# Windowed attention with a two-layer MLP: Q and K of two batches turned from 96 partitions, one block of tokens split in two

## The chip, the cores and the metric

The kernel runs on one core of a Trainium2 chip. The metric is the device time of one execution in microseconds (us). The median of several runs is compared with the median of the kernel before.

## What is computed

```python
def _attn_ref(q, k, v):                      # each (8, 8, 576, 64): batch, head, position, width
    scores = q @ k^T / sqrt(64)
    mask = |i - j| <= 32                     # a band of 65 positions
    attn = softmax(where(mask, scores, -1e9))
    return attn @ v

def reference(q, k, v, w_in, w_out, s, b):   # w_in (512, 2048), w_out (2048, 512)
    x = attention, heads side by side        # (4608, 512) tokens by model width
    r = max(x @ w_in, 0)
    return (s * r * r + b) @ w_out           # (4608, 512), float32
```

Inputs and output are float32; the kernel multiplies in bfloat16 and adds up in float32.

## The kernel before

**Order.** The program is a list of tasks, each for one engine, with a planned cost, a key and the tiles that it reads and writes. `_Graph.plan` simulates the engines and the DMA rings with these costs and writes down one fixed order for each engine; `emit` puts the semaphore waits in. Each engine then runs its list strictly in that order, so a task at the head of an engine's list that waits holds up all behind it. Tasks that write the same tile keep the order in which the program adds them.

**The start (batch 0).** SyncE issues eight loads of 288 KB (`load_pair`, line 579): Q and K of a pair of heads, one partition per nine positions of one head (`ROWS = 9`), so 128 partitions of 576 floats. Each load is cast to bfloat16 (`turn_pair`, lines 588 and 589: K on VectorE, Q on ScalarE or GpSimd), turned on TensorE by 18 transposes of 64x64 into a bank of `W` (line 595), and copied into `QT` by ScalarE (line 600) or `KT` by VectorE (line 601). `pair_scores` first writes the band's mask into the score bank with matmuls of an identity with `NEG` (line 817, two of 512 columns; for pair 0 also two in `AVN`, line 822), adds the scores of the pair (line 826, 18 matmuls on a quarter of the array) and lets ScalarE take the exponential (line 848). Before any of this, `WARM = 26` matmuls of 128x128 ones run on TensorE (line 486).

**Units.** Attention goes on in units of 128 rows: `av_part` (line 742, up to 32 matmuls of 64x64), `finish` (reciprocal 764, scaling 766, four transposes 773, copy into `XT` 781). Batch 0 has five units, batch 1 five; `BANK1` names the PSUM tile in which each unit of batch 1 gathers its result. From batch 2 on, Q and K are turned by DMA instead (lines 625 to 650).

**The MLP.** Tokens go in blocks (`sizes`): 96, 128, 128, 160 (the `NE = 4` early ones), then 512 each. For a block `s1` multiplies 128 columns of `w_in` at a time (line 973), ScalarE takes the ReLU (980) and VectorE the square (982). `group(m)` says how many chunks share a bank of `W`: four up to 128 tokens, two up to 256, one above. `s2` is the second layer (line 991; for the early blocks line 1022), 128 tokens at a time. The early blocks' `s1` are taken in the order of `FIRST`, weight group by weight group, as the weights arrive and GpSimd casts them (line 537). `attend(m)` adds attention tasks to the list until 1024 tokens past block `m` are made, so those of all of batch 1, and of batch 2 and part of 3, come into the list ahead of the `s1` of the first block of 512 (tokens 512 to 1023).

Of the kernel before, what the change touches and what calls it, by code (L numbers as in the profile page):

```python
# [11 lines left out]
S = 576  # L12
D = 64
# [19 lines left out]
          ("v", 0), ("v", 1), ("v", 2), ("v", 3), ("v", 4))  # L33
SWITCH = 215.0
XTS = 4000.0
ROWS = 9
XPE = 20
PACE = ((-1, -1, -1),) * 3
CASTS = 40.0
# [2 lines left out]
SLACK = (1000.0, 2000.0, 3000.0, 3000.0)  # L42
PACEV = ((-1,-1,0,0,1),(0,0,1,1,2),(0,0,1,1,2))
EV0 = ("pool", "dve", "pool", "dve", "pool")
BANK1 = ("W", "SC", "W", "SC", "AVN")
EV1 = ("pool", "pool", "pool", "pool", "pool")
EV2 = ("dve",) * 5

ACT_TABLE_SET_ID = 6
FAR = 1e38  # L50
TURN_DVE = ()
WARM = 26
LEAST = 2.0 ** -60
AHEAD = {"pe": 48, "act": 180, "dve": 240, "pool": 240}

# [16 lines left out]
class _Graph:  # L72
# [13 lines left out]
    def add(self, stream, fns, cost, reads=(), writes=(), key=0.0, accum=False, dma=None, waits=(),  # L86
            lat=None, slack=0.0):
        if not isinstance(fns, list):
            fns = [fns]
        after = [self.chain] if key < -100 and self.chain else []  # L90
        t = _Task(len(self.tasks), stream, fns, cost, self.LAT[stream] if lat is None else lat, key,
                  dma, slack, after)
        t.deps.update(waits)
        for a in after:
            assert a.stream == stream
            a.next.append(t)
        for r in reads:
            assert r in self.writer, r
            t.deps.add(self.writer[r])
        for w in writes:  # L100
            if w in self.writer:
                t.deps.add(self.writer[w])
            if not accum:
                t.deps.update(self.readers.get(w, ()))
        t.deps.discard(t)
        for r in reads:
            self.readers.setdefault(r, []).append(t)
        for w in writes:
            self.writer[w] = t
            if not accum:  # L110
                self.readers[w] = []
        self.tasks.append(t)
        if key < -100:
            self.chain = t
        return t
# [201 lines left out]
def bass_sliding_window_symmetric__then__act_starrelu_kernel(  # L317
# [10 lines left out]
    B = q.shape[0]  # L328
    T = B * S

    sizes = [96, 128, 128, 160]
    NE = len(sizes)
    while sum(sizes) < T:
        sizes.append(min(512, T - sum(sizes)))
    TBLK, t0 = [], 0
# [5 lines left out]
    with ExitStack() as es:  # L341
# [24 lines left out]
        STG = [STGS[:, i, :] for i in range(NSTG)]  # L366
        NATS = sb((128, NNAT, 2 * DM), BF16, "nat")
        NAT = [NATS[:, i, :] for i in range(NNAT)]
# [112 lines left out]
        for p0 in (0, 64):  # L481
# [1 line left out]

        add("pool", lambda e: e.tensor_scalar(NEG[:, :], MASK[:, :], 1.0, FAR, ALU.subtract, ALU.mult), 250,
            reads=[("MASK", 0, 0), ("MASK", 0, 64)], writes=["NEG"], key=-95.5)
        add("pe", [lambda e: e.matmul(W[:, 1, 0:128], lhsT=ONESW[:, :], rhs=ONESW[:, :], start=True, stop=True)] * WARM,
            110.0 * WARM, reads=["ONESW"], writes=[("W", 1)], key=-99)

        def mask_of(c, u):

# [84 lines left out]
        def load_pair(b, name, pr, load_key):  # L575

            si = take("stg", NSTG)
            land["pair", b, name, pr] = si
            add("sp", lambda e: e.dma_start(  # L579
                STG[si][:, 0:576],  # L580
                src_of[name][b, 2 * pr:2 * pr + 2, :, :].rearrange("h (p i) d -> (h p) (i d)", i=ROWS)),
                600.0, writes=[("STG", si)], key=load_key, dma=("l", 8, 113.0 if b == 0 else 93.0))

        def turn_pair(b, name, pr, key, banks, eng, slack):

            slot, si, ni = b % 2, land["pair", b, name, pr], take("nat", NNAT)
            nat = NAT[ni][:, 0:576]
            add(eng, (lambda e: e.copy(nat, STG[si][:, 0:576])) if eng == "act" else
                (lambda e: e.tensor_copy(nat, STG[si][:, 0:576])),
                {"act": 670.0, "dve": 420.0, "pool": 700.0}[eng], reads=[("STG", si)], writes=[("NAT", ni)],  # L590
                key=key, slack=slack)
            res, tile = banks[take("bank", len(banks))]
            view = tile.bitcast(BF16)[:, 0:S].rearrange("p (i s) -> p i s", i=ROWS)
            order = view.rearrange("p i s -> p s i")
            add("pe", [lambda e, i=i, p0=p0: e.transpose(  # L595
                view[p0:p0 + 64, i, :], nat[p0:p0 + 64, i * 64:i * 64 + 64], IDENT[p0:p0 + 64, p0:p0 + 64])
                for i in range(ROWS) for p0 in (0, 64)], 500.0, reads=[("NAT", ni), "IDENT"], writes=[res], key=key)
            flat = QT[slot][:, pr, WIN:WIN + S] if name == "q" else KT[slot][:, pr, :]
            dst = flat.rearrange("p (s i) -> p s i", i=ROWS)
            add(*(("act", lambda e: e.copy(dst, order), 190 + 0.833 * S) if name == "q" and (b, pr) not in TURN_DVE else  # L600
                  ("dve", lambda e: e.tensor_copy(dst, order), 60 + 1.04 * S)), reads=[res],
                writes=[({"q": "QT", "k": "KT"}[name], slot, x, pr) for x in range(NTILE)], key=key)
# [205 lines left out]
        def pair_scores(b, pr):  # L808


            name, bank = (("SC", SC), ("O", O))[pr % 2 if b == 0 else 0]
            whole = range(NTILE - NTILE % 2)
            tail = [NTILE - 1] if b == 0 and NTILE % 2 else []
            if b == 0:
                wide = NEG.rearrange("p (one c) -> p one c", one=1)
                four = wide.to_broadcast((128, 4, 128))
                add("pe", [lambda e, hp=hp: e.matmul(bank[:, hp, :].rearrange("p (a c) -> p a c", a=4), lhsT=IDENT[:, :],
                                                     rhs=four, start=True, stop=True, skip_group_check=True)
                           for hp in (0, 1)], 440, reads=["NEG", "IDENT"], writes=[(name, 0), (name, 1)], key=-80.0 + pr)
                if pr == 0:  # L820
                    half = wide[0:64].to_broadcast((64, 4, 128))
                    add("pe", [lambda e, hp=hp: e.matmul(
                        AVN[0:64, hp, :].rearrange("p (a c) -> p a c", a=4), lhsT=IDENT[0:64, 0:64],
                        rhs=half, start=True, stop=True, skip_group_check=True) for hp in (0, 1)],
                        440, reads=["NEG", "IDENT"], writes=[("AVN", 0), ("AVN", 1)], key=-79.5)
            fns = [lambda e, j=j, hp=hp: e.matmul(  # L826
                bank[64 * (j % 2):64 * (j % 2) + 64, hp, 64 * (j - j % 2):64 * (j - j % 2) + 128] if j in whole else
                AVN[0:64, hp, pr * 128:pr * 128 + 128],
                lhsT=KT[b][64 * hp:64 * hp + 64, pr, 64 * j:64 * j + 64],
                rhs=QT[b][64 * hp:64 * hp + 64, pr, 64 * j:64 * j + 128], start=b > 0, stop=True,  # L830
                skip_group_check=True)
                for j in list(whole) + tail for hp in (0, 1)]
# [52 lines left out]
        def attention():  # L885
# [41 lines left out]
            for u in range(NUNIT):  # L927
# [2 lines left out]
                    exp_mask(1, u, due(1, u) - 3.0)  # L930
                last.append((1, u))
                close()
            yield 2 * S
            for b in range(PAIRS, B):
                c = seq_of(b)
                later(b, due(c, group_of(b)[0]) - 24.0)
# [22 lines left out]
        def group(m):  # L959
            return 4 if TBLK[m][1] <= 128 else 2 if TBLK[m][1] <= 256 else 1  # L960
# [84 lines left out]

        def attend(m):
            nonlocal made
            while made < min(T, TBLK[m][0] + TBLK[m][1] + 1024):
                made = next(units)

        made = next(units)
# [2 lines left out]
                s1(m, ft)  # L1054
        early()
        attend(NE)
        for ft in range(16):
            s1(NE, ft)

        def second(m):  # L1060
# [3 lines left out]

        for m in range(NE + 1, NM):
            attend(m)
            for ft in range(16):
                s1(m, ft)
            second(m - 1)
        *rest, final = subs(NM - 1)  # L1070
# [249 lines left out]
```

## Time and profile before

| what | value |
|---|---|
| runs of the kernel | 318.11, 318.45, 319.67 us (median 318.45) |
| the profiled execution, its own time | 316.62 us |
| its span in the profile | 314.9 us |
| TensorE busy | 303.8 us (96%), 3559 matmuls and as many weight loads |
| VectorE, ScalarE, GpSimd busy | 189.6, 140.6, 90.5 us |
| DMA moved | 56.13 MB |

The span is what the profiler's records cover; the execution's own time has 1.7 us around it. "PE" is TensorE's matmuls, "PEld" its weight loads, "DVE" VectorE, "ACT" ScalarE, "POOL" GpSimd and "SP" SyncE. PEclk is the share of the clock that TensorE was granted.

### The profile page before, as it was taken

How to read it: one execution, taken by the hardware profiler on the slowest of the kernel's cores; microseconds unless marked ns; L12 is line 12 of the kernel's file. 1: busy time of each engine (PE TensorE's matmuls, PEld its weight loads, DVE VectorE, ACT ScalarE, POOL GpSimd, SP SyncE). 2: the span in 40 equal slices, each digit the busy share in tenths (PEclk: the TensorE clock that was granted, in tenths of full speed). 3: DMA queues.
4: the chain of work that ended last, by engine and by line, in shares of the span. 5: the costliest groups of instructions: out<-in, count | busy, mean ns of one | idle time of the engine just before them, and what ended most of it. 6: DMA issues, size and time to landing. Idle time of an engine off the chain costs nothing.

```text
span 314.9 us, 8371 instructions
## 1 busy us (share of the span) xinstructions
PE 303.8 (96%) x3559; PEld 158.6 (50%) x3559; DVE 189.6 (60%) x376; ACT 140.6 (45%) x219; POOL 90.5 (29%) x106
## 2 busy tenths in 40 slices
PE   7689999999999999999999999999999999999996
PEld 5478864544554544544444444444444444444444
DVE  2457686598886796686588666856455543333312
ACT  3636536257635765644354445444444333333300
POOL 7366853743334217142321601333000000000000
PEclk9959999999999999999999999999999999999999
DMA  7999999979998998999999799996211110010022
GB/s 252 296 278 392 386 311 301 187 151 312 233 152 242 242 165 199 287 162 139 269 225 186 180 220 291 143 181 129 72 54 52 52 46 34 33 37 33 34 88 83
DMA packets 98985, 56.13 MB, mean 178 GB/s; under 512 B 74048, under 2 KB 88128, under 8 KB 98944
## 3 DMA queue, kind: packets, MB, share of 16 engines
q1 hardware_dynamic: 98944, 55.56, 75.4%
q8 instruction: 29, 0.48, 0.7%
q14 instruction: 12, 0.10, 0.1%
HBM read 36.70 MB, written 9.44 MB: 147 GB/s over the span
## 4 chain that ended last, share of the span: by engine, by line
PE 86%; DMA 6%; DVE 3%; SPq 2%; issue 1%; ACT 1%
PE w L973 38%; PE o L991 33%; DMA stg<-in_k_dram 5%; PE avn L742 4%; PE o L1022 2%; PE avn L1022 2%; PE sc L684 2%; DMA vst<-in_v_dram 1%; SPq L625 1%; PE sc L742 1%; PE w L595 1%; PE avn L773 1%; SPq L579 1%; DVE xn L766 1%; PE sc L826 1%
## 5 line engine op out<-in xcount | busy, mean ns | idle before, releaser
L973 PE MATMUL w<-xt,win 128*128 128x512 bf16 (+3 forms) x768 | 145.5, 330 | 0.1
L980 ACT ACTIVATE r<-w 128x512 bf16<-128x512 f32 (+2 forms) x148 | 86.6, 586 | 104.9 <-PE w L973 90.9
L991 PE MATMUL o<-wout,gt 128*128 128x512 bf16 (+1 forms) x528 | 126.7, 373 | 0.0
L982 DVE TENSOR_TENSOR gt<-r 128x512 bf16<-128x512 bf16 (+2 forms) x148 | 77.4, 529 | 80.4 <-ACT r L980 79.7
L973 PEld LDWEIGHTS w<-xt,win 128*128 128x128 bf16 x768 | 63.5, 100 | 55.8 <-ACT r L980 0.8
L991 PEld LDWEIGHTS o<-wout,gt 128*128 128x128 bf16 x528 | 51.1, 98 | 57.3 <-DVE gt L982 0.2
L633 POOL CAST nat<-stg 128x1024 bf16<-128x1024 f32 (+1 forms) x21 | 25.3, 1204 | 64.6 <-DMA stg<-in_q_dram 47.8
L650 POOL COPY kt<-ktr 128x512 bf16<-128x512 bf16 (+1 forms) x30 | 31.8, 1060 | 38.2 <-DMA ktr<-nat 36.7
L712 ACT ACTIVATE ex<-sc 128x1024 bf16<-128x1024 f32 (+1 forms) x29 | 29.6, 1022 | 22.7 <-PE avn L742 21.6
L1007 DVE SCALAR_TENSOR_TENSOR outs<-o,sb,cvec 128x512 f32<-128x512 f32 (+1 forms) x35 | 25.4, 728 | 11.7 <-PE o L991 11.7
L716 DVE TENSOR_TENSOR ex<-ex,mask 128x1024 bf16<-128x1024 bf16 (+1 forms) x29 | 21.8, 752 | 1.1
L766 DVE TENSOR_TENSOR xn<-avn,rec 128x512 bf16<-128x512 f32 (+1 forms) x30 | 20.6, 688 | 0.9
L742 PE MATMUL avn<-vb,ex 64*64 64x65 bf16 x920 | 19.5, 199 | 0.7 <-DVE ex L716 0.5
L742 PEld LDWEIGHTS avn<-vb,ex 64*64 64x64 bf16 x920 | 12.7, 108 | 13.9 <-issue 6.1
L571 DVE CAST vb<-vst 128x512 bf16<-128x512 f32 (+1 forms) x30 | 12.9, 435 | 1.7 <-DMA vst<-in_v_dram 1.7
L633 DVE CAST nat<-stg 128x1024 bf16<-128x1024 f32 (+1 forms) x15 | 11.7, 786 | 1.2 <-DMA stg<-in_k_dram 1.2
L684 PE MATMUL sc<-qt,kt 64*64 64x128 bf16 x440 | 11.7, 216 | 0.7 <-ACT xt L781 0.7
L764 DVE RECIPROCAL rec<-avn 128x8 f32<-128x8 f32 (+1 forms) x30 | 6.0, 201 | 7.6 <-PE avn L742 7.3
L537 POOL CAST win<-stg 128x1024 bf16<-128x1024 f32 x8 | 8.4, 1049 | 6.4 <-DMA stg<-in_moe_w_in_dram 6.4
L537 POOL CAST wout<-stg 128x1024 bf16<-128x1024 f32 x8 | 8.8, 1100 | 2.0 <-DMA stg<-in_moe_w_out_dram 1.7
L781 ACT COPY xt<-avn 128x512 bf16<-128x512 bf16 (+2 forms) x13 | 6.6, 519 | 5.9 <-PE avn L773 5.9
L1022 PE MATMUL o<-wout,gt 128*128 128x512 bf16 x32 | 9.3, 381 | 0.0
(88 smaller groups left out, 143.0 us busy)
## 6 DMA issues: line engine op xcount, KB each, us to landing
out_dram<-outs SPq DMA_DIRECT2D x35, 256.0 KB, 2.9
vst<-in_v_dram SPq DMA_DIRECT2D x32, 256.0 KB, 6.6
stg<-in_q_dram SPq DMA_DIRECT2D x6, 1024.0 KB, 6.5
stg<-in_k_dram SPq DMA_DIRECT2D x6, 1024.0 KB, 10.8
stg<-in_moe_w_in_dram SPq DMA_DIRECT2D x8, 512.0 KB, 7.0
stg<-in_moe_w_out_dram SPq DMA_DIRECT2D x8, 512.0 KB, 9.7
stg<-in_q_dram SPq DMA_DIRECT2D x8, 288.0 KB, 5.5
stg<-in_k_dram SPq DMA_DIRECT2D x8, 288.0 KB, 5.4
```

Of the source, the lines that this page charges most:

```text
L633: add(eng, lambda e, x=x: e.tensor_copy(nat[0:top, 1024 * x:1024 * x + 1024].rearrange("p (i h d) -> p h i d", h=H, i=2), stg[0:top, :].re ...
L650: add("pool", lambda e, c=c, w=w: e.tensor_copy(KT[slot][:, :, c:c + w].rearrange("p a (s i) -> p a s i", i=4), KTR[slot][:, :, :, c // 4: ...
L712: add("act", lambda e, dst=flat_dst, src=flat_src: e.activation(dst, src, AF.Exp, bias=0.0, scale=0.125), 190 + 0.833 * 512 * len(hs), rea ...
L716: add("dve", lambda e, flat=flat, mask=mask: e.tensor_tensor(flat, flat, mask, ALU.mult), 130 + 0.53 * 512 * len(hs), reads=[("E", ei, hp, ...
L742: return [lambda e: e.matmul(av[64 * x:64 * x + 64, h, 0:D + 1], lhsT=buf[64 * g:64 * g + 64, h % 2, h // 2, c:c + 64], rhs=VB[64 * g:64 * ...
L766: add("dve", lambda e: e.tensor_tensor(XN[xi][0:p1, :].rearrange("p (a c) -> p a c", a=H), av[0:p1, :, 0:D], REC[ri][0:p1, :].rearrange("p ...
L973: add("pe", [lambda e, g=g, kc=kc: e.matmul(wt[:, g, :], lhsT=WIN_BF[:, kc, (f0 + g) * 128:(f0 + g + 1) * 128], rhs=XT[:, kc, t0 % XR:t0 % ...
L980: add("act", lambda e: e.activation(rt, wt, AF.Relu, bias=0.0, scale=1.0), 190 + 0.833 * ng * nt, reads=[("W", wb)], writes=[("R1", rb)], ...
L982: add("dve", lambda e: e.tensor_tensor(GT[gs][:, f0:f0 + ng, g0:g0 + nt], rt, rt, ALU.mult), 130 + 0.53 * ng * nt, reads=[("R1", rb)], wri ...
L991: add("pe", [lambda e, fc=fc: e.matmul(O[:, ob, 0:cn], lhsT=GT[gs][:, fc, g0:g0 + 128], rhs=WOUT_BF[:, fc, c0:c0 + cn], start=(fc == 0), s ...
L1007: add("dve", lambda e: e.scalar_tensor_tensor(OUTS[us][:, 0:cn], bank, SB128[:, 0:1], CVEC[:, c0:c0 + cn], ALU.mult, ALU.add), 200 + 1.07 ...
L1022: add("pe", [lambda e, fc=fc, bank=bank, gs=gs, g0=g0: e.matmul(bank, lhsT=GT[gs][:, fc, g0:g0 + 128], rhs=WOUT_BF[:, fc, :], start=(fc == ...
```

## The change

Four things are changed together.

1. `ROWS` is 6: Q and K of batches 0 and 1 lie in 96 partitions with both heads of the pair side by side, so a load has 192 pieces of 1536 bytes instead of 128 of 2304, a cast handles 96 x 768 elements instead of 128 x 576 and swaps two dimensions, and a turn is six transposes of 96 x 128 instead of 18 of 64 x 64.
2. The ones-matmuls at the start are five of 512 columns instead of 26 of 128.
3. The mask of pair `pr` (line 817) is kept behind the turn of K of pair `pr - 1`.
4. Tokens 512 to 1023 are two blocks of 256 (`NE` stays 4). The generator gives control back after each unit of batch 1, and the first block of 256 asks for no tokens past itself; units 2 and 3 of batch 1 gather in `SC` and `AVN` instead of `W` and `SC`.

```diff
-ROWS = 9
+ROWS = 6
-BANK1 = ("W", "SC", "W", "SC", "AVN")
+BANK1 = ("W", "SC", "SC", "AVN", "AVN")
-WARM = 26
+WARM = 5
...
-    sizes = [96, 128, 128, 160]
-    NE = len(sizes)
+    sizes = [96, 128, 128, 160, 256, 256]
+    NE = 4
...
-        add("pe", [lambda e: e.matmul(W[:, 1, 0:128], lhsT=ONESW[:, :], rhs=ONESW[:, :], start=True, stop=True)] * WARM,
-            110.0 * WARM, reads=["ONESW"], writes=[("W", 1)], key=-99)
+        ones = ONESW.rearrange("p (one c) -> p one c", one=1).to_broadcast((128, 4, 128))
+        add("pe", [lambda e: e.matmul(W[:, 1, :].rearrange("p (a c) -> p a c", a=4), lhsT=ONESW[:, :], rhs=ones,
+                                      start=True, stop=True)] * WARM,
+            430.0 * WARM, reads=["ONESW"], writes=[("W", 1)], key=-99)
...
-                STG[si][:, 0:576],
-                src_of[name][b, 2 * pr:2 * pr + 2, :, :].rearrange("h (p i) d -> (h p) (i d)", i=ROWS)),
-                600.0, writes=[("STG", si)], key=load_key, dma=("l", 8, 113.0 if b == 0 else 93.0))
+                STG[si][0:S // ROWS, 0:2 * ROWS * D].rearrange("p (h c) -> p h c", h=2),
+                src_of[name][b, 2 * pr:2 * pr + 2, :, :].rearrange("h (p i) d -> p h (i d)", i=ROWS)),
+                600.0, writes=[("STG", si)], key=load_key, dma=("l", 12, 75.0 if b == 0 else 62.0))
...
-            add("pe", [lambda e, i=i, p0=p0: e.transpose(
-                view[p0:p0 + 64, i, :], nat[p0:p0 + 64, i * 64:i * 64 + 64], IDENT[p0:p0 + 64, p0:p0 + 64])
-                for i in range(ROWS) for p0 in (0, 64)], 500.0, reads=[("NAT", ni), "IDENT"], writes=[res], key=key)
+            add("pe", [lambda e, i=i: e.transpose(view[:, i, :], nat[:, i, :], IDENT[0:np_, 0:np_])
+                       for i in range(ROWS)], 300.0 if b else 400.0, reads=[("NAT", ni), "IDENT"], writes=[res], key=key)
+            land["turn", b, name, pr] = g.tasks[-1]
...
                            for hp in (0, 1)], 440, reads=["NEG", "IDENT"], writes=[(name, 0), (name, 1)], key=-80.0 + pr,
+                    waits=[land["turn", 0, "k", pr - 1]] if pr else [])
...
-            yield 2 * S
+                yield closed[0]
...
-            while made < min(T, TBLK[m][0] + TBLK[m][1] + 1024):
+            while made < min(T, TBLK[m][0] + TBLK[m][1] + (1024 if m > NE else 0)):
                 made = next(units)
...
-        for ft in range(16):
+        for ft in range(0, 16, group(NE)):
             s1(NE, ft)
...
-            for ft in range(16):
+            for ft in range(0, 16, group(m)):
                 s1(m, ft)
```

The casts' planned costs are adapted as well (830, 560 and 930 ns for ScalarE, VectorE and GpSimd).

More of the change, by code (lines that the diff above doesn't have):

```diff
@@ L579, in load_pair @@
             add("sp", lambda e: e.dma_start(
-                STG[si][:, 0:576],
-                src_of[name][b, 2 * pr:2 * pr + 2, :, :].rearrange("h (p i) d -> (h p) (i d)", i=ROWS)),
-                600.0, writes=[("STG", si)], key=load_key, dma=("l", 8, 113.0 if b == 0 else 93.0))
+                STG[si][0:S // ROWS, 0:2 * ROWS * D].rearrange("p (h c) -> p h c", h=2),
+                src_of[name][b, 2 * pr:2 * pr + 2, :, :].rearrange("h (p i) d -> p h (i d)", i=ROWS)),
+                600.0, writes=[("STG", si)], key=load_key, dma=("l", 12, 75.0 if b == 0 else 62.0))
         def turn_pair(b, name, pr, key, banks, eng, slack):
             slot, si, ni = b % 2, land["pair", b, name, pr], take("nat", NNAT)
[L587 to L590, printed above, removed]
+            np_, n = S // ROWS, 2 * ROWS * D
+            nat = NAT[ni][0:np_, 0:n].rearrange("p (i c) -> p i c", i=ROWS)
+            dst = NAT[ni][0:np_, 0:n].rearrange("p (i h d) -> p h i d", i=ROWS, h=2)
+            src = STG[si][0:np_, 0:n].rearrange("p (h i d) -> p h i d", i=ROWS, h=2)
+            add(eng, (lambda e, dst=dst, src=src: e.copy(dst, src)) if eng == "act" else
+                (lambda e, dst=dst, src=src: e.tensor_copy(dst, src)),
+                {"act": 830.0, "dve": 560.0, "pool": 930.0}[eng], reads=[("STG", si)], writes=[("NAT", ni)],
                 key=key, slack=slack)
@@ L818, in pair_scores @@
                                                      rhs=four, start=True, stop=True, skip_group_check=True)
-                           for hp in (0, 1)], 440, reads=["NEG", "IDENT"], writes=[(name, 0), (name, 1)], key=-80.0 + pr)
+                           for hp in (0, 1)], 440, reads=["NEG", "IDENT"], writes=[(name, 0), (name, 1)], key=-80.0 + pr,
+                    waits=[land["turn", 0, "k", pr - 1]] if pr else [])
                 if pr == 0:
```

## The prediction

> **What bounds the kernel now.** I read the page first, then the chain of waits, then the windows view of the start, and the timeline where the chain has holes.
>
> From the page:
>
> ```profile
> PE 303.8 (96%) x3559; PEld 158.6 (50%) x3559; DVE 189.6 (60%) x376; ACT 140.6 (45%) x219; POOL 90.5 (29%) x106
> ...
> PEclk9959999999999999999999999999999999999999
> ...
> q8 instruction: 29, 0.48, 0.7%
> ```
>
> TensorE is the bound. It is without work for only 314.9 - 303.8 = 11.1 us, and one slice, the third (15.7 to 23.6 us), ran at half clock. What can be won lies there. The chain of waits, beginning and end of the start:
>
> ```profile
> 3.14 5.41 DMA stg<-in_k_dram
> ...
> 11.93 1.65 issue
> 13.59 0.31 PE sc L826 x8
> ...
> 19.65 1.39 PE w L973 x16
> ...
> 64.90 0.41 PE sc L684 x8
> ```
>
> The loads of Q and K set the pace up to 8.6 us; then there are 1.65 us of "issue", in which TensorE waits for nothing that the profile shows; from 18 us on the chain is nearly all TensorE. The windows view, cut where the clock changes and into thirds of the 10.24 us between two changes:
>
> ```profile
> core 0: us, PE busy (x) PEld busy (x) DVE busy (x) ACT busy (x) POOL busy (x), PEclk, DMA share, GB/s
> 0.00:11.93 11.93, 9.00 (x222) 6.49 (x222) 4.89 (x17) 5.99 (x8) 7.46 (x24) 1.00 0.87 264
> 1.22:4.64 3.42, 2.89 (x27) 2.62 (x28) 0.74 (x7) 1.54 (x2) 2.85 (x9) 1.00 0.78 254
> 4.64:8.05 3.41, 2.81 (x60) 1.36 (x60) 1.25 (x3) 0.69 (x2) 2.35 (x9) 1.00 0.98 347
> 8.05:11.46 3.41, 2.73 (x116) 2.09 (x118) 2.52 (x5) 2.87 (x4) 1.30 (x3) 1.00 1.15 280
> 11.46:14.88 3.42, 1.76 (x56) 0.92 (x54) 1.09 (x2) 1.62 (x3) 0.88 (x2) 1.00 1.04 313
> 14.88:25.12 10.24, 8.87 (x190) 7.05 (x191) 5.25 (x11) 4.65 (x9) 6.67 (x9) 0.50 1.03 293
> 25.12:35.36 10.24, 10.11 (x164) 9.21 (x163) 7.40 (x16) 6.54 (x13) 7.46 (x7) 1.00 1.05 390
> ```
>
> The clock falls to 0.50 at 14.88 us and comes back at 25.12. The first window's 1.00 is not to be believed: the timeline has 26 ones-matmuls of 128 columns in 2.96 us, 110 ns each, where 128 columns later take 56 (below). So TensorE began at half clock, and the ones raised it near 4.64 us. The DMA share near 1 says that the loads are at their limit until 64 us.
>
> ```profile
> 1.12 2.96 PE L486 MATMUL w<-onesw 128*128 128x128 bf16 x26 [1.12 <-DVE onesw L463]
> ...
> 13.59 0.31 PE L826 MATMUL sc<-qt,kt 64*64 64x128 bf16 x8 [1.65 <-issue]
> ...
> 42.75 0.76 PE L595 MATMUL w<-ident,nat 64*64 64x64 bf16 x36
> 43.44 0.60 PE L1022 MATMUL avn<-wout,gt 128*128 128x512 bf16 x2
> ...
> 64.90 0.41 PE L684 MATMUL sc<-qt,kt 64*64 64x128 bf16 x8 [0.68 <-ACT xt L781]
> 65.25 2.76 PE L973 MATMUL w<-xt,win 128*128 128x512 bf16 x12
> ```
>
> **The change part by part.** All sums are against the profiled execution, 316.62 us with a span of 314.9.
>
> *The turns themselves: nothing.* At full clock 36 transposes of 64x64 start within 43.44 - 42.75 = 0.69 us, 19 ns each because two run side by side, 0.345 us a turn. Six whole-array ones go at the rate of line 773, four between 59.45 and 59.68 in the chain, 55 to 58 ns: 0.34 us. The count falls (16 turns x 12 = 192 fewer matmuls, as many weight loads), the time does not. The copies out of `W` keep their size (0.64 and 0.75 us).
>
> *Fewer instructions before the gap: -1.65 us.* The gap comes after 222 matmuls and 222 weight loads, in the middle of one task. The page has 29 instruction packets for 7118 TensorE rows, about 245 a packet, so I read it as the wait for a packet of code, asked for while the loads fill the DMA engines. The change takes 21 ones and, in the eight turns, 96 matmuls away before this point, 234 rows with their loads. The 444th row then lies in the third unit's matmuls (line 742, 18.70 us now), some 7 us later, while the packet starts at most a few us later. Bounds: 0 (the gap reappears there) to -1.65; I take -1.65.
>
> *The cold stretch.* I read the rows so that the clock goes by how much of the array works. I weigh each matmul's columns by its share of the 128x128 array. 11.46 to 14.88 holds 36 score matmuls (a quarter of 128 columns: 1152), two mask matmuls (1024) and 18 transposes (a quarter of 64: 288), 2464 of some 8190 that fit into 3.41 us (512 in 216 ns is about 2400 a us), 0.30; after it the clock fell. The same count gives 0.32 and 0.42 for the two windows before, and there it stayed. At half clock (4096 columns) 18.29 to 21.70 has 0.69 and did not raise it, 21.70 to 25.12 has 0.78 and did, and 25 ones (3200) gave 0.78. After the change the stretch of the fall holds the same scores and mask, a turn of 12 x 96 columns x 0.75 = 864 and, the gap being gone, the first unit's 24 matmuls (390): 3430, 0.42, where it stayed. At full clock the work of 14.88 to 25.12 shrinks: 32 matmuls of line 742 from 0.95 to 0.70 (x4.5: 1.1), four transposes of line 773 from 0.61 to 0.39 (x3.5: 0.8), the two groups of line 973 from 1.46 and 1.89 to about 1.0 each (1.4): 3.3 us.
>
> [...]
>
> *The cap.* Gap and clock together are 4.95 us, but the weights come no sooner. Casts of `w_in` (GpSimd, line 537, idle before each for the DMA) end at 17.4, 23.3, 27.4 and 30.1 us for the four groups; their first uses are at 19.6, 26.3, about 31 and 36.8. The second group allows 3.0 us. So -3.0.
>
> *Loads and casts of 96 partitions.* The eight loads are 2.36 MB, 6.2 us at the 380 GB/s of 6 to 8 us; the 2 KB pieces of the weights ran at 390 (25.12 to 35.36). Pieces of 1.5 KB I bound from 0 to 10% worse, 0 to +0.6 us for all that follows; I take +0.3. K's last cast grows from 0.46 to 0.61 (768 to 576 elements), +0.15, on the path to the last scores. Q's on GpSimd grow by 0.2 beside it.
>
> *The moved masks: 0.* Line 817 of pair 1 (0.53 us) leaves the place ahead of the first turns; the third K load, landing at 8.55, ends last there. Behind its wait stand only scores that need the same turn. Without this cover it would cost 0.53.
>
> *Two blocks of 256.* 64 matmuls of 512 columns become 128 of 256. The chain has eight of 160 columns in 0.55 us (69 ns each) and four of 512 in 0.86 (216 ns), so a fixed part of some 2 ns lies in each, 64 times 2 ns or 0.15 us. Banks still hold 512 columns, so ScalarE's 597 ns and VectorE's 516 come as often. `s1` of the first half needs two units of batch 1, not four: the 0.68 us before 64.90 and 0.32 near 46.5 can be filled. -0.3 to -1.0; I take -0.8. From 66 us on the same work runs on a busy TensorE.
>
> *Given back.* At 41 to 47 us casts of batch 1's Q and K wait for DMA (0.4 to 0.8 us each). TensorE, earlier by up to 3.0, can meet them in its fixed order, with line 1022 as cover. 0 to +3.0; I take +0.5, because line 1022's 64 matmuls (13.8 us) are mostly still to do then.
>
> Sum: -3.0 + 0.3 + 0.15 + 0.15 - 0.8 + 0.5 = -2.7 us, 313.9 on the profiled execution. That one lies 1.8 under the median 318.45 of the runs, and the place of the clock's windows, which differs from run to run, may be why. I put the sum on the median: 315.7, 312.6 to 316.9 with the bounds (low: -4.0 on 316.62).
>
> **The rivals.** *The clock rises late (slower).* Five ones are 2560 columns, 0.62 of 4096: less than the 0.69 that did not raise it. The masks and whole-array turns from 4.6 us on may do it (at half clock 1024 + 256 + 864 + some 600 by 8.05: 0.67) or miss again. It decides if the clock is still at half at about 11.5 us, since then TensorE, not the loads, is behind: five pairs of masks at 0.85, 48 transposes at 110 ns, four times 18 score matmuls at 0.9: 4.3 + 5.3 + 3.7 = 13.2 us from 4.6, 17.8 against the end of the scores at 14.8 now, +3.0. With the other terms 318.45 + 3.0 + 0.6 - 0.8 = 321.2, or 319.4 on the profiled execution. For it: the 0.62. Against it: denser turns, and late rises in the runs of before too.
>
> [...]
>
> *The gap goes, the clock falls as now.* -1.65 + 0.6 - 0.8 + 0.5 = -1.35: 317.1.
>
> *The loads hide it all.* If pieces of 1.5 KB cost the whole 0.6 us and batch 1's loads take the rest back, only the filled holes stay, -0.8 + 0.6: 318.3. This is also the case in which the new turns change nothing.
>
> **How the numbers follow.** Forecast 0.48, gap only 0.22, late clock 0.16, loads 0.14. A difference under 0.5% (1.6 us) cannot be told from none here. Faster (under 316.9): 0.46 of the forecast's and half of the second rival, whose bounds lie on both sides, 0.57. Same: the other half, the loads and a little of the late clock, 0.28. Slower (over 320.0): 0.15. The range 312.8 to 319.8 leaves out the worst of the late clock and the forecast's edge.
>
> **What would show it.** Right: no "issue" of over 1 us before 15 us; PEclk without the 5 in the third slice; the first line 973 group at about 17.5 us and the second weight group's at 23.5; the first 256-wide line 973 rows near 57 us; no new wait of TensorE after 66. Wrong: line 595 matmuls 110 ns apart up to 12 us, scores of pair 3 ending after 15 us, a gap inside line 742 near 18, or TensorE idle for DMA between 40 and 48 us.

## The result and the profile after

| kernel | median of the runs (us) | range | profiled execution, its span |
|---|---|---|---|
| before | 318.54 (4 runs) | 318.11 to 319.67 | 316.62, 314.9 |
| after | 323.61 (4 runs) | 322.12 to 324.12 | 322.12, 320.3 |

The ratio is 1.0146, with an interval of 1.0101 to 1.019: slower by 1.5%, where 315.7 was forecast, and outside the range of 312.8 to 319.8. Ratios here compare runs timed beside each other, without the few that lie over 1.5% above the fastest of their kernel, so they differ a little from the quotient of the medians.

The page of the kernel after: busy time, clock, instruction packets, the chain by engine, and the issues of Q and K of batches 0 and 1 (count, KB each, median us from issue to landing).

```profile
PE 300.6 (94%) x3365; PEld 163.8 (51%) x3410; DVE 192.3 (60%) x376; ACT 140.9 (44%) x219; POOL 94.6 (30%) x106
...
PEclk9857999999999999999999999999999999999999
...
q8 instruction: 28, 0.46, 0.6%
...
PE 74%; DMA 17%; DVE 3%; issue 2%; SPq 1%; POOL 1%; ACT 1%; DVEq 0%
...
stg<-in_q_dram SPq DMA_DIRECT2D x8, 288.0 KB, 8.1
stg<-in_k_dram SPq DMA_DIRECT2D x8, 288.0 KB, 7.6
```

The same rows of before, for loads of the same 288 KB:

```profile
stg<-in_q_dram SPq DMA_DIRECT2D x8, 288.0 KB, 5.5
stg<-in_k_dram SPq DMA_DIRECT2D x8, 288.0 KB, 5.4
```

So a load takes 2.2 to 2.6 us longer from issue to landing, and the share of DMA on the chain has nearly tripled (before has 86% PE and 6% DMA there). (That share alone proves little: the kernel with wide loads below has 13% and about the time of before.) (45 matmul records are missing here, 3365 against 3410 weight loads; the idle pieces of 0.16 us beside groups of seven matmuls come from that, and some of the lower PE share with them.)

The chain of the waits of after, from the stretches 0 to 30 us and 40 to 110 us (start, duration, what):

```profile
4.21 8.92 DMA stg<-in_k_dram
...
13.15 0.56 DVE nat L594
13.71 0.68 DVE kt L606
...
14.43 0.66 PE w L600 x6
...
41.06 9.21 DMA stg<-in_k_dram
...
50.30 0.56 DVE nat L594
50.85 0.67 DVE cvec L1045
...
51.57 0.42 PE sc L832 x16
```

In before, the chain left the DMA at 8.55 us. Here it stays on a load of K until 13.1, and goes back to one from 41 to 50 us. The windows view of 2 to 12 us shows what those loads got; its last two columns are the DMA share and the GB/s. First before, then after:

```profile
2.00:12.00 10.00, 8.13 (x216) 5.60 (x213) 4.06 (x9) 4.86 (x8) 6.30 (x18) 1.00 1.03 314
```

```profile
2.00:12.00 10.00, 8.23 (x62) 3.65 (x61) 3.04 (x6) 3.86 (x6) 5.57 (x17) 1.00 1.05 251
```

The DMA engines are as busy (1.03 and 1.05) and move a fifth less. How the delay goes on is seen from VectorE's casts of K, TensorE's first matmuls of a kind, and the first load of batch 2:

| event | before (us) | after (us) | later by |
|---|---|---|---|
| last cast of K, batch 0 | 10.17 | 13.15 | 3.0 |
| first `s1` matmuls (line 973 before, 979 after) | 19.58 | 22.10 | 2.5 |
| first scores of batch 1 | 46.78 | 51.57 | 4.8 |
| last cast of K, batch 1 | 46.65 | 52.54 | 5.9 |
| first load of batch 2 issued | 47.84 | 54.29 | 6.5 |
| end | 314.9 | 320.3 | 5.4 |

The timeline of TensorE after (start, duration, operation, count, idle time before it):

```profile
1.12 2.32 PE L487 MATMUL w<-onesw 128*128 128x512 bf16 x5 [1.12 <-DVE onesw L463]
...
14.43 0.66 PE L600 MATMUL w<-ident,nat 96*128 96x96 bf16 x6 [1.23 <-DVE kt L606]
...
51.57 0.42 PE L832 MATMUL sc<-qt,kt 64*64 64x128 bf16 x16 [1.09 <-DVE cvec L1045]
...
97.71 0.40 PE L778 MATMUL avn<-ident,xn 128*128 128x128 bf16 x4 [1.02 <-DVE xn L771]
...
103.22 1.90 PE L979 MATMUL w<-xt,win 128*128 128x512 bf16 x8 [0.68 <-ACT xt L786]
...
105.88 0.25 PE L747 MATMUL avn<-vb,ex 64*64 64x65 bf16 x6 [0.76 <-POOL kt L655]
```

Three waits stand near 100 us (1.02, 0.68 and 0.76 us). From 66 to 110 us TensorE was busy for 43.89 of 44 us before and for 40.37 after:

```profile
66.00:110.00 44.00, 43.89 (x540) 21.49 (x539) 34.80 (x63) 27.16 (x43) 16.07 (x16) 1.00 1.00 224
```

```profile
66.00:110.00 44.00, 40.37 (x568) 26.44 (x564) 33.99 (x60) 22.99 (x36) 20.27 (x19) 1.00 0.97 209
```

Of the 3.5 us between the two, the three waits are 2.5; most of the rest is the idle pieces of eight matmuls that are missing from the records in this stretch. So some of the loss shows far behind the place where the change was made. What causes these waits is not shown: batch 2's loads were issued 6.5 us late, but two of the three waits stand also in the kernel with wide loads below, whose batch 2 was issued in time.

How the loads of batch 2 come late is seen from SyncE's queue after:

```profile
34.27 0.33 SPq L581 DMA_DIRECT2D stg<-in_q_dram  x1
...
45.23 8.97 SPq L564 DMA_DIRECT2D vst<-in_v_dram  x5
54.29 0.56 SPq L630 DMA_DIRECT2D stg<-in_q_dram  x1
```

The first load of batch 1 goes out at 34.27 us (31.41 in before), behind the weights. The last load of batch 1 goes out at 44.87 us (40.91 in before). Behind all eight stand five loads of V, which take 8.97 us on the queue, until 54.2 us (6.46 us in before, until 47.7); the longest of the five takes 4.97 us (47.11 to 52.08), and the profile names nothing that released it. Only then comes batch 2.

### The profile page after: what moved, and what is told of

It is laid out like the page before. It is cut to its first block, busy times and chain, and to the rows that moved or that the text cites. A ratio compares the mean times of both kernels' runs of the same rounds, so it can differ in the third digit from the quotient of the medians.

```text
span 320.3 us, 8026 instructions
## 1 busy us (share of the span) xinstructions
PE 300.6 (94%) x3365; PEld 163.8 (51%) x3410; DVE 192.3 (60%) x376; ACT 140.9 (44%) x219; POOL 94.6 (30%) x106
## 4 chain that ended last, share of the span: by engine, by line
PE 74%; DMA 17%; DVE 3%; issue 2%; SPq 1%; POOL 1%; ACT 1%; DVEq 0%
PE w L979 32%; PE o L997 31%; DMA stg<-in_k_dram 9%; PE avn L747 3%; DMA stg<-in_moe_w_out_dram 3%; DMA stg<-in_moe_w_in_dram 3%; DMA ktr<-nat 2%; PE sc L689 2%; PE avn L1028 1%; PE o L1028 1%; SPq L581 1%; PE sc L747 1%; PE sc L832 1%; PE w L600 1%; DVE outs L1013 1%
## 5 line engine op out<-in xcount | busy, mean ns | idle before, releaser
L979 PE MATMUL w<-xt,win 128*128 128x512 bf16 (+4 forms) x813 | 141.1, 315 | 3.7 <-issue 1.4
L997 PE MATMUL o<-wout,gt 128*128 128x512 bf16 (+1 forms) x510 | 122.8, 372 | 2.1 <-issue 1.6
L979 PEld LDWEIGHTS w<-xt,win 128*128 128x128 bf16 x832 | 70.3, 99 | 54.0 <-ACT xt L786 0.8
L997 PEld LDWEIGHTS o<-wout,gt 128*128 128x128 bf16 x528 | 50.4, 98 | 54.8
L655 POOL COPY kt<-ktr 128x512 bf16<-128x512 bf16 (+1 forms) x30 | 32.9, 1097 | 44.4 <-DMA ktr<-nat 42.9
L717 ACT ACTIVATE ex<-sc 128x1024 bf16<-128x1024 f32 (+1 forms) x29 | 29.7, 1023 | 22.7 <-PE avn L747 21.8
L1013 DVE SCALAR_TENSOR_TENSOR outs<-o,sb,cvec 128x512 f32<-128x512 f32 (+1 forms) x35 | 25.4, 729 | 13.2 <-PE o L997 12.9
L771 DVE TENSOR_TENSOR xn<-avn,rec 128x512 bf16<-128x512 f32 (+1 forms) x31 | 21.4, 689 | 0.9
L747 PEld LDWEIGHTS avn<-vb,ex 64*64 64x64 bf16 x952 | 13.1, 108 | 14.1 <-issue 7.0
L573 DVE CAST vb<-vst 128x512 bf16<-128x512 f32 (+1 forms) x30 | 15.2, 505 | 2.4 <-DMA vst<-in_v_dram 2.2
L594 DVE CAST nat<-stg 96x768 bf16<-96x768 f32 x8 | 4.4, 554 | 9.7 <-DMA stg<-in_k_dram 9.7
## 6 DMA issues: line engine op xcount, KB each, us to landing
stg<-in_moe_w_out_dram SPq DMA_DIRECT2D x8, 512.0 KB, 10.2
```

The costliest lines, as they stand in the source:

```text
L655: add("pool", lambda e, c=c, w=w: e.tensor_copy(KT[slot][:, :, c:c + w].rearrange("p a (s i) -> p a s i", i=4), KTR[slot][:, :, :, c // 4: ...
L717: add("act", lambda e, dst=flat_dst, src=flat_src: e.activation(dst, src, AF.Exp, bias=0.0, scale=0.125), 190 + 0.833 * 512 * len(hs), rea ...
L747: return [lambda e: e.matmul(av[64 * x:64 * x + 64, h, 0:D + 1], lhsT=buf[64 * g:64 * g + 64, h % 2, h // 2, c:c + 64], rhs=VB[64 * g:64 * ...
L771: add("dve", lambda e: e.tensor_tensor(XN[xi][0:p1, :].rearrange("p (a c) -> p a c", a=H), av[0:p1, :, 0:D], REC[ri][0:p1, :].rearrange("p ...
L979: add("pe", [lambda e, g=g, kc=kc: e.matmul(wt[:, g, :], lhsT=WIN_BF[:, kc, (f0 + g) * 128:(f0 + g + 1) * 128], rhs=XT[:, kc, t0 % XR:t0 % ...
L997: add("pe", [lambda e, fc=fc: e.matmul(O[:, ob, 0:cn], lhsT=GT[gs][:, fc, g0:g0 + 128], rhs=WOUT_BF[:, fc, c0:c0 + cn], start=(fc == 0), s ...
```

## The experiments

**Theory:** a load into 96 partitions moves fewer bytes a second than one into 128, whatever the size of its pieces, and it sets the pace at both batches. **Rivals:** the pieces of 1536 bytes are to blame; the casts and turns in the new layout; the clock, which rose late (in after only at 10.25 us, and it was back at half from 13.67 to 27.32, 13.65 us against 10.24 in before); the split with its other banks. All ratios are to the kernel before, timed on the same chip beside each. Differences of medians between two changed kernels cross chips; where they matter the difference of the ratios stands beside them.

The long stretch of half clock does not explain the loss. The mean granted clock of the four runs of after is 0.979 in the profiled one (322.12 us) and 0.989 in the other three, the same as in the profiled run of the nine-row kernel below; these three took 323.18 to 324.12 us, longer than the profiled one.

### The loads by themselves

A kernel that does nothing but load Q's and K's first batches, 16 loads of 288 KB in each of eight phases, with a wait between the phases.

```diff
+ phase 1, 8: 128 partitions, one piece of 2304 B        STG[:, 0:576]
+ phase 2:    96 partitions, two pieces of 1536 B        STG[0:96, 0:768], "h (p i) d -> p h (i d)"
+ phase 3:    96 partitions, one piece of 3072 B         STG[0:96, 0:768]
+ phase 4:    128 partitions, two pieces of 1152 B, 128 B apart
+ phase 5:    as phase 2, in partitions 32 to 127
+ phase 6:    two DMAs of 32 partitions (0-31, 32-63), 4608 B each
+ phase 7:    two DMAs of 32 partitions (0-31, 64-95), 4608 B each
```

> This kernel only loads; attention and the MLP are left out. Eight phases, each the 16 loads of 288 KB of Q and K of batches 0 and 1, each phase waiting for the one before: (1) 128 partitions, pieces of 2304 bytes; (2) partitions 0 to 95, two pieces of 1536; (3) partitions 0 to 95, one piece of 3072; (4) 128 partitions, two pieces of 1152; (5) partitions 32 to 127, two of 1536; (6) partitions 0 to 31 and 32 to 63, pieces of 4608; (7) partitions 0 to 31 and 64 to 95, pieces of 4608; (8) as (1). Theory, the number and place of the partitions set the rate: phases 1, 4 and 8 some 380 GB/s (12.4 us for 4.72 MB), phases 2, 3 and 5 all near 270 (17.5 us), phase 6 about half of phase 1, phase 7 near phase 1. Rival, the size of the pieces sets it: phase 2 and 5 near 270, phase 3 near 400, phase 4 the slowest of the first five (about 220), phases 6 and 7 both near 400.

The windows of that kernel, one in the middle of each phase (the last two columns are DMA share and GB/s):

```profile
core 0: us, POOL busy (x), PEclk, DMA share, GB/s
4.00:12.00 8.00, 0.00 (x0) 1.00 1.00 364
20.00:32.00 12.00, 0.00 (x0) 1.00 1.09 244
41.00:53.00 12.00, 0.00 (x0) 1.00 1.02 270
61.00:67.00 6.00, 0.00 (x0) 1.00 1.03 331
77.00:91.00 14.00, 0.00 (x0) 1.00 1.07 249
97.00:115.00 18.00, 0.00 (x0) 1.00 1.03 214
119.00:135.00 16.00, 0.00 (x0) 1.00 0.93 240
143.00:151.00 8.00, 0.00 (x0) 1.00 0.99 367
```

Over whole phases (4.72 MB by the time from the phase's first packet to the end of its last) the eight ran at 333, 238, 261, 324, 236, 211, 250 and 334 GB/s. The second phase is the load of the change, the first that of before: 238 against 333, or 1.40 times as long. Pieces of 1152 bytes in 128 partitions hardly lose (324), one piece of 3072 in 96 partitions does (261): the number of partitions decides, and two pieces in place of one cost about a tenth more within 96. The seventh phase missed its expectation: two DMAs of 32 partitions in different halves got 250, not the rate of 128; the same two in one half (the sixth phase) got 211.

### The loads, by halves of the partitions

The same with other places, to see why 96 is slow.

```diff
+ phase 1: 128 partitions, one DMA
+ phase 2: 64 partitions (0-63), one DMA      phase 3: 64 partitions (64-127), one DMA
+ phase 4: four DMAs of 16 partitions at 0, 64, 16, 80
+ phase 5: four DMAs of 16 partitions at 0, 32, 16, 48
+ phase 6: two DMAs of 64 partitions (0-63, 64-127)
```

> Loads only again (attention and the MLP are left out), 16 of 288 KB a phase: (1) 128 partitions, one DMA a load; (2) partitions 0 to 63; (3) 64 to 127; (4) partitions 0-15, 64-79, 16-31, 80-95 as four DMAs of 16; (5) partitions 0-15, 32-47, 16-31, 48-63 as four DMAs of 16; (6) 0 to 63 and 64 to 127 as two DMAs. [...] Rival, the rate goes with the number of partitions alone: (2) to (5) all between 211 and 250, (6) as (1).

Over whole phases: 348, 205, 206, 155, 126 and 225 GB/s. The windows of phases 1, 2, 3:

```profile
4.00:12.00 8.00, 0.00 (x0) 1.00 1.00 370
20.00:34.00 14.00, 0.00 (x0) 1.00 1.02 209
44.00:58.00 14.00, 0.00 (x0) 1.00 1.03 212
```

Either half of the partitions alone gets 0.59 of the rate of all (205 and 206 of 348). Two DMAs, one to each half, do not add up (225): of these six, only the one DMA across all partitions gets 348. The fourth and fifth phases missed the author's estimates (155 and 126, where 300 or more and 211 were estimated): DMAs of 16 partitions were slow in both places. That the place counts, and not the number of partitions alone, is seen from pairs with equal DMAs in both halves and in one: 155 / 126 = 1.23 here, 250 / 211 = 1.18 in the run before.

At the 205 GB/s of one half, the two thirds of a load into 96 partitions that lie in one half would let the whole run at 205 / (2/3) = 307 GB/s, if the last third cost no time beside them: an estimate from the 205 alone. Measured are 238 and 261, so by this estimate the rate of one half does not explain all of it. What the rest is, no run here shows.

### The changed kernel with the old rows

```diff
 (after)
-ROWS = 6
+ROWS = 9
+load_pair and turn_pair as before: 128 partitions of 576, 18 transposes of 64x64
```

> The changed kernel with its loads, casts and turns of Q and K put back to nine rows in 128 partitions; ones, moved masks and two blocks of 256 stay. Theory, the slower loads of 96 partitions cost the time (k of pair 3 landed 3 us later, and the same again for batch 1): back by 4 to 6 us to 317.5 to 319.5, last K cast of batch 0 at 10.2 us. Rival, the clock's late rise after the shorter ones: the start stays late, first group of the first layer after 21 us, 321.5 to 323.5. Rival, the split of the block makes the waits of TensorE seen between 95 and 106 us: these stay, 320.5 to 322.

Measured: 316.95 us (316.34 to 317.91, 10 runs), ratio 0.9954 (0.992 to 0.9989). Its windows row of 2 to 12 us, the issues of its page, and the wait for K of batch 1 in its timeline:

```profile
2.00:12.00 10.00, 8.65 (x148) 4.52 (x148) 3.28 (x7) 3.53 (x6) 6.19 (x18) 1.00 1.01 302
```

```profile
stg<-in_q_dram SPq DMA_DIRECT2D x8, 288.0 KB, 5.7
stg<-in_k_dram SPq DMA_DIRECT2D x8, 288.0 KB, 5.9
```

```profile
47.40 0.42 PE L830 MATMUL sc<-qt,kt 64*64 64x128 bf16 x16 [0.35 <-DVE cvec L1043]
```

The rows take the whole loss with them and more: 323.61 - 316.95 = 6.7 us, or 6.1 by the ratios; that is better than the theory's range. The last cast of K starts at 10.91 us, against 13.15 in after (10.2 was expected). The three waits near 100 us are gone too, and TensorE is busy for 43.93 of the 44 us from 66 to 110. Its clock rose at 11.24 us only, fell at 18.07 and came back at 24.90, and it is still quicker than before: the late rise is not what cost the time.

### The kernel before with the new rows alone

```diff
 (before)
-ROWS = 9
+ROWS = 6
+load_pair and turn_pair of the change; 26 ones, masks, blocks and banks as before
```

> The kernel before with loads, casts and turns of Q and K from 96 partitions, nothing else changed. Theory of the loads: 322.5 to 324.5, last K cast of batch 0 near 13 us. Rival of the clock: 318 to 319.5 (26 ones are still there). Rival of the split: 318 to 319.5.

Measured: 326.68 us (323.33 to 327.8, 4 runs), ratio 1.0247 (1.0151 to 1.0344). The last cast of K starts at 12.78 us, the first scores of batch 1 wait 1.23 us (1.09 in after):

```profile
12.78 0.56 DVE L592 CAST nat<-stg 96x768 bf16<-96x768 f32 x1 [0.62 <-DMA stg<-in_k_dram]
```

```profile
51.29 0.42 PE L829 MATMUL sc<-qt,kt 64*64 64x128 bf16 x16 [1.23 <-DVE cvec L1042]
```

The rows alone cost 8.1 us on the kernel before, more than the 5.1 of the whole change and more than the theory's range (322.5 to 324.5). The 26 ones that were kept do not prevent it. In the profiled execution the clock fell a second time, from 68.04 to 74.86 us, after waits of TensorE of 0.79, 0.44 and 0.68 us. That fall does not explain the surplus: the mean granted clock is 0.979 in three of the four runs, but the fourth, with 0.989, took 327.80 us, the longest. Why the rows cost more here than in the changed kernel is not shown.

### The changed kernel with wide loads only

The casts and turns stay those of the change (96 x 768, six transposes); only the DMA writes 128 partitions of 576, which puts the values of Q and K into other places.

```diff
 (after)
-STG[si][0:96, 0:768] <- "h (p i) d -> p h (i d)", i=6
+STG[si][:, 0:576]    <- "h (p i) d -> (h p) (i d)", i=9
+memset of STG columns 576:768, once, at the start
```

> The changed kernel, but its loads of Q and K fill 128 partitions with pieces of 2304 bytes as before; casts and turns still work on 96 partitions of 768 elements, so the values of Q and K stand in the wrong places and the rest of each row is zero or old data; the eight small memsets for the zeros lie on an idle VectorE. Theory, the landing of the loads alone costs the time: 316.5 to 318.5, last K cast of batch 0 near 10.3 us. Rival, the longer casts (0.56 and 0.82 us) and the turns carry part of it: 319.5 to 322 with a last K cast near 10.3 us all the same.

Measured: 317.7 us (316.55 to 319.43, 10 runs), ratio 0.998 (0.9951 to 1.0009). From its windows, issues and VectorE's timeline:

```profile
2.00:12.00 10.00, 8.78 (x65) 4.27 (x64) 5.45 (x17) 3.85 (x6) 6.68 (x18) 1.00 1.02 302
```

```profile
stg<-in_q_dram SPq DMA_DIRECT2D x8, 288.0 KB, 5.7
stg<-in_k_dram SPq DMA_DIRECT2D x8, 288.0 KB, 5.7
```

```profile
11.02 0.55 DVE L596 CAST nat<-stg 96x768 bf16<-96x768 f32 x1
```

The landing alone is worth 323.61 - 317.7 = 5.9 of the 6.7 us (5.3 of 6.1 by the ratios). For the new casts and turns (and the memsets that this kernel adds) 0.8 us are left, and the intervals of the two runs overlap. The profiled execution is the slowest of the ten, 319.43 us. In it batch 2's first load goes out at 47.56 us, as early as in before (47.84), and two of the three waits near 100 us are there all the same:

```profile
98.72 1.90 PE L981 MATMUL w<-xt,win 128*128 128x512 bf16 x8 [0.68 <-ACT xt L788]
101.40 0.25 PE L749 MATMUL avn<-vb,ex 64*64 64x65 bf16 x6 [0.78 <-POOL kt L657]
```

One thing was not tried. The plan of after prices a load of batch 0 at 12 x 75 = 900 ns, where before has 8 x 113 = 904, so the engines' fixed orders were made for loads as quick as before. How much of the 5.9 us an order made for the slower loads would save is open.

### Old rows for batch 0 only

```diff
 (after)
+if b == 0: load and turn as in the kernel before (nine rows); else: six rows
```

> The changed kernel with nine rows in 128 partitions for batch 0 alone; batch 1 still loads into 96 partitions. Theory, both batches' loads delay TensorE, each by some 3 us: 319 to 321. Rival, only the start counts since batch 1's loads are hidden behind the early blocks: 316.5 to 318. Rival, the start is made up for later and only batch 1 counts: 322 to 324.

Measured: 320.32 us (318.38 to 324.01, 10 runs), ratio 1.0052 (1.0016 to 1.0088): 3.3 us under after, 3.4 over nine rows in both batches (3.0 and 3.1 by the ratios). The last cast of K of batch 0 is back at 10.36 us, but TensorE still waits for batch 1:

```profile
49.37 0.42 PE L868 MATMUL sc<-qt,kt 64*64 64x128 bf16 x16 [1.56 <-DVE cvec L1081]
```

So each batch pays about half.

### The split alone

```diff
 (before)
-BANK1 = ("W", "SC", "W", "SC", "AVN")
+BANK1 = ("W", "SC", "SC", "AVN", "AVN")
-sizes = [96, 128, 128, 160]
+sizes = [96, 128, 128, 160, 256, 256]     # NE = 4, and part 4 of the change
```

> The kernel before with tokens 512 to 1023 as two blocks of 256, control given back after each unit of batch 1, and the new banks; loads, ones and masks as before. Theory of the loads: 317.5 to 318.8, since the split alone only fills holes near 64 us (at most 1 us). Rival of the split: 320.5 to 322 with waits of TensorE of 0.5 us and more between 90 and 110 us. Rival of the clock: 318 to 319.

Measured: 318.93 us (316.41 to 320.18, 10 runs), ratio 1.0031 (0.9998 to 1.0065). The 0.8 us expected of it do not show, and neither does the rival's loss of 2 us and more. The gap stands at its old place, after 222 matmuls, but is short, since TensorE came to it 1.3 us later (clock up at 10.56 us only, although it had 26 ones); a second one of 0.59 us follows at 19.90, after 348:

```profile
13.48 0.31 PE L826 MATMUL sc<-qt,kt 64*64 64x128 bf16 x8 [0.21 <-issue]
```

### The start: masks, ones, and both

Three kernels from before, one with the moved masks, one with five long ones, one with both; a fourth from the nine-row kernel with eight ones.

```diff
 (before_masks)          +waits=[land["turn", 0, "k", pr - 1]] on line 817
 (before_five_ones)      -WARM = 26 (128 columns)   +WARM = 5 (512 columns)
 (before_ones_and_masks) both
 (nine_rows_eight_ones)  in after with nine rows:  -WARM = 5   +WARM = 8
```

> The kernel before with the masks kept behind the turns of K, nothing else. Theory, TensorE's 0.53 us move off the place ahead of the first turn but the loads end last there: 317.5 to 318.6, no difference that can be told. Rival, the moved masks are what made the nine-row version faster: 316.5 to 317.3.

> The kernel before with the five long ones-matmuls alone. Theory of the loads: 317.5 to 318.8, no difference that can be told, as the clock rose late with 26 ones too (10.6 and 16.8 us in two runs). Rival of the clock: 319.5 to 321.

> The kernel before with the five long ones-matmuls and the masks kept behind the turns of K; no split, nine rows. Theory of the loads: these two parts are worth 0 to 2 us, 316.5 to 318.5, since everything but the loads gained 1.6 us. Rival of the clock: too few ones, 319.5 to 321.

> The changed kernel with nine rows in 128 partitions and eight long ones-matmuls instead of five (3.4 us at half clock, ending just before the first masks). If an early rise of the clock is worth something it rises near 4.6 us in more runs: 315 to 316.5. If the rise is only shifted with the fall that follows 7 to 10 us later: as with five, 316.5 to 317.5.

The first rise of the clock is read from the spacing of equal matmuls, the rest from the granted clock of the windows.

| kernel | median (us), runs | ratio | clock up, down, up (us) | gap |
|---|---|---|---|---|
| masks | 319.5, 12 | 1.0025 (0.9993 to 1.0057) | 4.19, 14.43, 24.67 | 1.29 after 222 matmuls |
| five ones | 320.27, 12 | 1.0045 (1.0007 to 1.0082) | 16.16, 23.0, 26.4 | 1.68 after 348 |
| ones and masks | 318.44, 12 | 1.0013 (0.9983 to 1.0044) | 10.30, 17.13, 23.96 | none before 25 us |
| nine rows, eight ones | 318.38, 12 | 0.9986 (0.9951 to 1.0021) | 5.72, 15.96, 22.78 | 0.52 after 221 |

The gaps, from the timelines of the masks, the five ones and the eight ones, and a later one from that of ones and masks:

```profile
13.30 0.31 PE L828 MATMUL sc<-qt,kt 64*64 64x128 bf16 x8 [1.29 <-issue]
```

```profile
23.07 0.38 PE L744 MATMUL sc<-vb,ex 64*64 64x65 bf16 x11 [1.68 <-issue]
```

```profile
13.83 0.36 PE L830 MATMUL o<-qt,kt 64*64 64x128 bf16 x11 [0.52 <-issue]
```

```profile
63.36 0.21 PE L745 MATMUL sc<-vb,ex 64*64 64x65 bf16 x1 [1.82 <-issue]
```

The gap goes by the number of instructions, not by the place in the program: with as many weight loads as matmuls it comes after 222 matmuls, or after 348, 252 instructions further, and with the eight ones it comes at another matmul of the program than before. With the other recorded instructions of TensorE's stream counted too (semaphores and one drain: in before 5 of them stand beside the 222 matmuls and weight loads, 9 beside the first 348), that is 449 and 705 instructions, 256 apart. There are later pauses: 0.34 us at 47.53 (the split alone), 0.45 at 64.98 (five ones) and 1.82 at 63.36 (ones and masks). The first gap was 1.65 us long where TensorE got to it at 11.93, 1.29 at 12.0, and 0.52 and 0.21 at 13.3. In before a packet of 16384 bytes on the instruction queue takes from 10.90 to 12.09 us, and TensorE goes on at 13.59, 1.50 us after its end; that TensorE waits for this packet is the author's reading. Before has 29 instruction packets and one pause of over 0.2 us, so most of its packets came without a pause of that length, but single pauses took up to 1.8 us in these runs.

The masks alone and the five ones alone took longer than expected. Five ones alone are a little slower than 26, and 320.27 us lies in the range of the rival, the clock (319.5 to 321): the clock of that profile rose only at 16.16 us. So a rise as late as that may have cost something; it is not shown apart from the gap of 1.68 us in the same profile. With the masks moved as well, the time is that of before. And an early rise is no gain that could be seen: eight ones raised the clock 5.5 us earlier than in the nine-row kernel with five, and it fell 2.1 us earlier; that kernel is not quicker, and its median lies above both expected ranges.

### Nine rows with the old ones

The rest of the change, that is the split and the moved masks, on the rows and ones of before.

```diff
 (after with nine rows)
-WARM = 5 (512 columns)
+WARM = 26 (128 columns)
```

> The changed kernel with nine rows in 128 partitions and with the 26 short ones back; so the kernel before with the split and the moved masks. Theory, the five ones bring nothing or cost up to 1 us (alone they made 1.0045): 315.5 to 317. Rival, fewer instructions ahead of the gap are what made the nine-row version faster: 317.5 to 318.8, with a wait of TensorE for nothing visible after some 222 matmuls.

Measured: 317.25 us (315.2 to 320.92, 12 runs), ratio 0.9954 (0.9919 to 0.9988). That lies between the theory's range and the rival's, and its trace has no pause of over 0.2 us after 222 matmuls, so that part of the rival is out (one of 1.34 us comes at 88.56). This kernel and the nine-row kernel with five ones are quicker than before and after; over before it is half a per cent. The split alone (1.0031) and the masks alone (1.0025) gain nothing; why the two together do was not found.

## Why the prediction was wrong, step by step

- **Loads and casts of 96 partitions (+0.3, at most +0.6; K's cast +0.15): this step failed.** It looked at the size of the pieces alone and took the number of partitions to be free. The loads by themselves take 1.40 times as long, of which the piece is a small part. In the kernel that is +3.0 us at the last cast of K of batch 0 and as much again at batch 1, and about 5.9 us of the total by the wide loads, where the sum had 0.3. K's cast itself was rightly sized (0.56 measured, 0.61 predicted). The trace of before had no load into 96 partitions, so the upper bound of this unknown should have been taken from rows with other numbers of partitions, or left wide. The gains at the start could not count, since the loads set its pace.
- **The gap (-1.65): right in what it goes by, worth nothing.** The pause does go by the number of instructions (449 and 705 ahead of it), and no "issue" of over 0.2 us is left at the start of after. But TensorE waits at 14.43 us behind the load of K instead (1.23 us), so what was saved went into that wait.
- **The cold stretch: failed.** In after the clock fell at 13.67 us, after a window that the weighing puts at 0.35, where the rows of before had it stay at 0.32; it came back at 27.32, later than the 25.12 of before. Every profile shows such a fall and return, whatever was put at the start. The weighing by columns does not hold: in ones and masks the clock fell after a window of 0.34, in five ones it stayed after one of 0.31. Nor does plain busy time: it fell after 2.47 us of matmuls in 3.41 (the split alone, from 13.97 us) and stayed after 1.59 (ones and masks, from 61.51 us). Leaving the transposes out does not help either: so counted, it stayed after 0.22 in before (4.64 to 8.05 us) and fell after 0.31 in ones and masks. What makes it fall stays open.
- **The cap of 3.0 by the casts of `w_in`: never reached.** The first matmuls of line 979 came 2.5 us later, not earlier.
- **The turns (0): right.** In the chain of after, six transposes at full clock take 0.36 us (54.59 to 54.96), 0.34 was worked out; fewer matmuls, no time.
- **The moved masks (0): right within what can be told** (1.0025 alone, 1.0013 with the ones).
- **The split (-0.8): not shown.** Alone it gives 1.0031; its cost of +0.15 for smaller matmuls is too small to be seen.
- **Given back (+0.5, bounds 0 to +3.0): wrong size, and another cause.** Batch 1's waits for DMA were expected as TensorE coming earlier; they came as loads landing later. The first scores of batch 1 are 4.8 us later.
- **"From 66 us on the same work runs on a busy TensorE": wrong.** New waits of 1.02, 0.68 and 0.76 us stand near 100 us in after. Batch 2's loads, behind those of batch 1 and of V in SyncE's queue, went out 6.5 us late, but with the wide loads they went out in time and two of the waits stayed (0.68 and 0.78 us); with nine rows all are gone. Their cause is not shown.
- **The rivals.** The only slower one was the late clock, 321.2 us. The clock did rise late (10.25 us), but the nine-row kernel has a later rise and no loss: right side, wrong cause. "The loads hide it all" named the right part and put it at 0.6 us. No rival had the loads themselves lose more than everything else gains, though they set the pace up to 8.6 us.
- **The sums.** The rival of the late clock has 3.7 us for four times 18 scores at 0.9, which is 3.6; its 13.2 us is right with that. The upper end of the forecast's bounds, 316.9, does not come from its terms: with all of them at their upper bounds the sum is -3.0 + 0.6 + 0.15 + 0.15 - 0.3 + 3.0 = +0.6 us, 319.05 on the median. Even that is 4.6 us under the measured time.

Of the prediction's signs of being wrong, two held in after: the scores of pair 3 end at 17.4 us, and TensorE waits between 40 and 48 us (0.69 us at 44.90 for a cast of `w_out`, 0.26 at 46.59 for a cast of Q or K). The longer wait, 1.09 us, ends at 51.57, behind that stretch. The 5 in the third slice of PEclk, which was to go, stayed.

## What to carry to other kernels

When a change alters the number of partitions that a DMA writes, that number is a term of the sum by itself: 288 KB into 96 or 64 partitions took 1.3 to 1.7 times as long here as into 128, with the DMA engines just as busy (shares of 1.02 to 1.09), so a DMA share near 1 must be read beside the GB/s. A saving on TensorE in the stretch whose pace the loads set was worth nothing here: the gap of 1.65 us went, and a wait of 1.23 us behind a load of K came. Loads that looked hidden behind other work were not free: batch 1's, in the middle of the early blocks, cost as much as batch 0's at the start. Where the trace of before shows no row for a new kind of transfer, its bound must be wide enough to reach the other side of the sum.

## What was not expected of the hardware

- 128 partitions in one DMA: 333 to 348 GB/s; 96: 236 to 261; 64: 205; one DMA to each half, together: 225. The 205 of one half, taken alone, would still allow 307 for 96 partitions (an estimate, 205 / (2/3)).
- TensorE paused after 449 recorded instructions in before (1.65 us) and after 705 with five ones (1.68 us), and the program's place of the first pause moved with the number of ones; the pauses told above took 0.21 to 1.82 us. In before TensorE went on 1.50 us after a 16384-byte packet of the instruction queue had ended.
- The granted clock fell to half between 13.7 and 23.0 us and returned between 22.8 and 27.3 us in every profile, whatever the ones at the start; with 26 ones it had risen at 4.64, 10.56, 4.19, 10.14 and 16.84 us. Getting it up 5 us earlier (eight ones against five, nine rows) gained nothing that could be measured.
